# A VectorE exp built from four tensors instead of three, in a kernel that adds attention and a gated MLP

## Chip, cores, metric

One core of a Trainium2 chip. The experiments ran on several chips; each is compared with the kernel before on its own chip, in the same rounds. The metric is the time on the device in microseconds (us), median of several executions. Engines: PE is TensorE (PEld its weight load), DVE is VectorE, ACT is ScalarE, POOL is GpSimd.

## The reference

```python
def _A_ref(x, wqkv, wo):                    # x: 1 x 2048 x 512, 32 heads of 16
    qkv = (x @ wqkv).reshape(B, S, 3, H, Dh).transpose(2, 0, 3, 1, 4)
    scores = einsum("bhqd,bhkd->bhqk", q, k) * (Dh ** -0.5)
    p = softmax(scores)
    return (p @ v).transpose(...).reshape(B, S, D) @ wo
def _B_ref(x, W_gate, W_up, W_down):        # inner width 1792
    return (relu(x @ W_gate) * (x @ W_up)) @ W_down
xn = layernorm(x)
return x + _A_ref(xn, ...) + _B_ref(xn, ...)
```

There are 32 x 2048 x 2048 exps, cut into 2048 tiles of 128 x 512. Nothing else in the program is as large.

## The kernel before

The program describes all its work as operations with durations, priorities and dependencies; a list scheduler in the kernel puts them in one fixed order per engine, and the order is then emitted. A change of a duration, a count or a constant therefore gives a new order of everything.

ACT does the exp of most tiles, in units of alternately three and two tiles, from five PSUM banks that TensorE fills with scores:

```python
SIZES = (3, 2)
...
G.op("PE", 225, sc, mode="row", rows=[t[4] for t in cl], reads=rd, writes=[ts], prio=u - 2000, ...)
...
return e.activation(ring[:, a:a + n, :], ps_sc[:, 3 * k0:3 * k0 + n, :], ACTF.Exp, scale=0.25)
```

98 groups of four tiles go to VectorE, which builds exp from the bits of a bf16 number. Each d1 turns one tile of scores into a bit pattern; d2 to d5 work on the group at once:

```python
# d1, four times: pattern = score * a + b, written as uint16
e.tensor_scalar(dring[:, tr.slot, 0, 512*j:512*j+512].bitcast(U16), ps_b[:, 2, :], 0.25*LOG2E*128.0, ..., op0=ALU.mult, op1=ALU.add)
# d2: mantissa, d3: exponent with a small constant, d4: mantissa squared, d5: pattern times the square
e.tensor_scalar(b(2, U16), b(0, U16), 0x7F, 0x3F80, op0=ALU.bitwise_and, op1=ALU.bitwise_or)
e.tensor_scalar(b(1, U16), b(0, U16), 0xFF80, N_MANT, op0=ALU.bitwise_and, op1=ALU.bitwise_or)
e.tensor_tensor(b(2, FP16), b(2), b(2), ALU.mult)
e.tensor_tensor(b(2), b(0), b(2, FP16), ALU.mult)
```

The weighted sum of the three tensors is never formed. TensorE multiplies each with its own scaled copy of v and adds them in PSUM, so such a group costs it three PV steps (probabilities times v; one step is four column-tiled matmuls), where a group of ACT's costs one. Holes in TensorE's order are filled with dummy matmuls on zeros.

The softmax here doesn't subtract the row's maximum and nothing guards it: scores larger than these inputs give would overflow.

## Time and profile before

| | before |
|---|---|
| time, median | 784.8 us (784.17 to 785.02) |
| profiled span, mean clock | 781.5 us, 0.999 |
| busy PE / DVE / ACT | 757.5 / 734.8 / 762.6 us |

A line of the costliest groups gives source line, engine, operation, out<-in with shapes and count; then busy time and the mean ns of one; then the idle time before them and what ended most of it. The stage lines give, for a stretch in us, each engine's busy time and count, the clock, the DMA share and GB/s. The prediction below shows both.

### The profile page before, as it was taken

The page shows a single profiled execution, that of the slowest core. Times are in us where ns is not written, and L with a number is a line of the kernel's source. Part 1 is how long each engine was busy: PE and PEld are TensorE (multiplying, and loading weights), DVE is VectorE, ACT ScalarE, POOL GpSimd, SP SyncE. Part 2 cuts the span into 40 slices and gives each one's busy share as a digit, 9 for nine tenths or more (in the row PEclk, how much of TensorE's full clock was granted, in tenths as well). Part 3 has the DMA queues.
Part 4 walks back from the last instruction along what each step waited for, and adds up shares of the span by engine and source line. Part 5 has one row for each costly group of instructions (what it writes and reads, how often), then busy time and mean ns, then how long its engine had stood idle before and what let it go on. Part 6 is the DMA issues. An engine that isn't in the chain of part 4 may idle for free.

```text
span 781.5 us, 20994 instructions
## 1 busy us (share of the span) xinstructions
PE 757.5 (97%) x9226; PEld 225.6 (29%) x9226; DVE 734.8 (94%) x1068; ACT 762.6 (98%) x678; POOL 165.5 (21%) x172
## 2 busy tenths in 40 slices
PE   8999999999999999999999999999999999999997
PEld 3322222222222222222222222222222232322232
DVE  8689999999999999999999899999999998999894
ACT  6999999999999999999999999999999999999995
POOL 3111122220222213121222021222021131221200
PEclk9999999999999999999999999999999999999999
DMA  7312121212220132221221113121213113321100
GB/s 215 111 40 71 41 65 41 63 36 66 53 76 23 43 83 56 64 53 47 68 57 56 42 43 84 42 74 38 70 41 83 49 29 96 78 76 43 31 20 28
DMA packets 95755, 46.80 MB, mean 60 GB/s; under 512 B 69936, under 2 KB 91824, under 8 KB 95664
## 3 DMA queue, kind: packets, MB, share of 16 engines
q1 hardware_dynamic: 95664, 45.46, 21.5%
q8 instruction: 72, 1.18, 0.6%
q14 instruction: 19, 0.16, 0.1%
HBM read 36.70 MB, written 8.50 MB: 58 GB/s over the span
## 4 chain that ended last, share of the span: by engine, by line
DVE 52%; PE 35%; ACT 10%; DMA 1%; issue 1%; POOL 0%; DVEq 0%; SPq 0%
DVE dring L1193 17%; PE ps_b L707 13%; ACT ring L1245 10%; PE ps_sc L1177 9%; DVE dring L1209 8%; PE ps_b L1153 8%; DVE dring L1210 8%; DVE dring L1205 4%; DVE dring L1207 4%; DVE up_sb L923 3%; PE ps_b L1177 3%; DVE hT L927 3%; DVE Wv L1089 1%; PE ps_b L1295 1%; DVE stats L616 1%
## 5 line engine op out<-in xcount | busy, mean ns | idle before, releaser
L1245 ACT ACTIVATE ring<-ps_sc 128x1536 bf16<-128x1536 f32 (+1 forms) x663 | 754.4, 1281 | 2.9 <-PE ps_sc L1177 1.4
L1193 DVE TENSOR_SCALAR dring<-ps_b 128x512 uint16<-128x512 f32 x392 | 267.3, 682 | 20.7 <-PE ps_b L1177 20.3
L1177 PE MATMUL ps_sc<-qm,kT 32*128 32x512 bf16 x1656 | 263.8, 384 | 6.0 <-ACT ring L1245 3.5
L1177 PE MATMUL ps_b<-qm,kT 32*128 32x512 bf16 x392 | 150.0, 383 | 5.6 <-DVE dring L1193 3.3
L1153 PE MATMUL ps_b<-ring,v_aug 128*17 128x512 bf16 x1656 | 149.2, 382 | 2.2 <-DVE Wv L1089 1.2
L1107 POOL TENSOR_TENSOR rrec<-rsum,minus 128x16 f32<-128x16 f32 x30 | 100.2, 3341 | 229.1 <-DMA rsum<-Wv 229.1
L1177 PEld LDWEIGHTS ps_sc<-qm,kT 32*128 32x128 bf16 x1656 | 63.5, 91 | 233.3 <-ACT ring L1245 203.9
L1210 DVE TENSOR_TENSOR dring<-dring 128x2048 bf16<-128x2048 bf16 x98 | 118.9, 1213 | 0.1
L1209 DVE TENSOR_TENSOR dring<-dring 128x2048 f16<-128x2048 bf16 x98 | 118.9, 1213 | 0.0
L1117 POOL TENSOR_TENSOR x_sb<-Wv,rb 128x128 bf16<-128x128 f32 x100 | 45.7, 457 | 280.0 <-DVE dring L1207 89.8
L707 PE MATMUL ps_b<-xnT,wus 128*32 128x512 bf16 x896 | 69.1, 384 | 0.8 <-DVE hT L927 0.2
L1205 DVE TENSOR_SCALAR dring<-dring 128x2048 uint16<-128x2048 uint16 x98 | 67.3, 687 | 1.5
L707 PE MATMUL ps_b<-xnT,wgs 128*32 128x512 bf16 x896 | 67.6, 384 | 0.4 <-DVE up_sb L923 0.2
L1207 DVE TENSOR_SCALAR dring<-dring 128x2048 uint16<-128x2048 uint16 x98 | 66.9, 683 | 0.0
L1153 PE MATMUL ps_b<-dring,vd 128*17 128x512 bf16 x784 | 64.9, 381 | 0.0
L707 PE MATMUL ps_b<-Wd,hT 128*32 128x512 bf16 x768 | 58.9, 382 | 0.1
L1153 PEld LDWEIGHTS ps_b<-ring,v_aug 128*17 128x17 bf16 x1656 | 36.9, 89 | 68.2 <-issue 50.1
L1177 PEld LDWEIGHTS ps_b<-qm,kT 32*128 32x128 bf16 x392 | 35.6, 91 | 57.9 <-DVE dring L1193 43.8
L923 DVE COPY up_sb<-ps_b 128x512 f32<-128x512 f32 x56 | 38.1, 680 | 1.8 <-PE ps_b L707 1.8
L1153 PE MATMUL ps_b<-dring,v_aug 128*17 128x512 bf16 x392 | 38.5, 383 | 1.3 <-DVE dring L1207 0.6
L1295 PE MATMUL ps_b<-zeros 128*17 128x512 bf16 x460 | 39.1, 381 | 0.0
L927 DVE SCALAR_TENSOR_TENSOR hT<-ps_b,up_sb 128x512 bf16<-128x512 f32 x48 | 32.7, 680 | 0.0
(106 smaller groups left out, 356.2 us busy)
## 6 DMA issues: line engine op xcount, KB each, us to landing
rb<-rec_scr SPq DMA_DIRECT2D x30, 256.0 KB
wus<-in_B_W_up_dram SPq DMA_DIRECT2D x56, 128.0 KB, 3.5
wgs<-in_B_W_gate_dram SPq DMA_DIRECT2D x56, 128.0 KB, 2.3
qm<-q_scr SPq DMA_DIRECT2D x30, 128.0 KB
o_scr<-x_sb SPq DMA_DIRECT2D x25, 128.0 KB
q_scr<-qT SPq DMA_DIRECT2D x17, 128.0 KB
xr_sb<-in_A_x_dram SPq DMA_DIRECT2D x16, 128.0 KB, 2.8
out_dram<-xn_sb SPq DMA_DIRECT2D x16, 128.0 KB, 1.7
```

What stands on the lines that cost most here:

```text
L707: ins = e.matmul(bank_of(tile, sub)[32 * j:32 * j + 32, :], st[:, 32 * j:32 * j + 32], mv, start=(i == 0), stop=(i == n - 1), tile_positio ...
L923: G.op("DVE", 610, lambda e: e.tensor_copy(up_sb[:, tup.slot, :], bank_of(tu)), reads=[tu], writes=[tup], prio=slots[1] + EV)
L927: G.op("DVE", 610, lambda e: e.scalar_tensor_tensor(out=h_of(th), in0=bank_of(tg), scalar=0.0, in1=up_sb[:, tup.slot, :], op0=ALU.max, op1 ...
L1107: G.op("POOL", 3000, lambda e: e.tensor_tensor(rrec[:, par, :], rsum[:, par, :], minus[:, 0:1].to_broadcast([128, 16]), ALU.pow), reads=[t ...
L1153: ins = e.matmul(ps_b[32 * j:32 * j + VN, 0, :], v, src[j][1](k), start=(first and k == 0), stop=(last and (k == 2 or not on)), tile_posit ...
L1177: return e.matmul(bank, kT[32 * j:32 * j + 32, gg, 128 * kt:128 * kt + 128], qm[32 * j:32 * j + 32, t_q[(c4, gg)].slot, ee, :], start=True ...
L1193: o = G.op("DVE", 610, lambda e, j=j: e.tensor_scalar(dring[:, tr.slot, 0, 512 * j:512 * j + 512].bitcast(U16), ps_b[:, 2, :], 0.25 * LOG2 ...
L1205: G.op("DVE", 600, lambda e: e.tensor_scalar(b(2, U16), b(0, U16), 0x7F, 0x3F80, op0=ALU.bitwise_and, op1=ALU.bitwise_or), reads=[tr], wri ...
L1207: G.op("DVE", 600, lambda e: e.tensor_scalar(b(1, U16), b(0, U16), 0xFF80, N_MANT, op0=ALU.bitwise_and, op1=ALU.bitwise_or), reads=[tr], w ...
L1209: G.op("DVE", 1140, lambda e: e.tensor_tensor(b(2, FP16), b(2), b(2), ALU.mult), reads=[tm], writes=[tm], prio=u - 3, name="d4", lock=True)
L1210: G.op("DVE", 1140, lambda e: e.tensor_tensor(b(2), b(0), b(2, FP16), ALU.mult), reads=[tm, tr], writes=[tm], prio=u - 3, name="d5", lock= ...
L1245: return e.activation(ring[:, a:a + n, :], ps_sc[:, 3 * k0:3 * k0 + n, :], ACTF.Exp, scale=0.25)
```

## The change

The intent: drop the squaring, one of the two dear two-input operations, by using the raw mantissa integer as a factor, and pay for the accuracy with a fourth cheap tensor and a fourth PV step. The freed VectorE time takes six more groups from ACT (98 to 104).

```diff
-NDR = 3
+NDR = 9
-D_GROUPS = 98
-D_SKIP = 12
+D_GROUPS = 104
+D_SKIP = 10
-O_LAST = 58
+O_LAST = 70
-EV = -940.0
-PACE_L = 1.2
+EV = -20.0
+PACE_L = 1.1
...
-    SLIP = 200.0
-    KEEP = 6.0
-    RIDE = 40.0
+    SLIP = 60.0
+    KEEP = 4.0
+    RIDE = 70.0
...
-        dring = sb("dring", [128, NDR, 3, 4 * 512], BF16)
+        dring = sb("dring", [128, NDR, 4 * 512], BF16)
...
-            for k in range(3 if on else 1):
+            ways = len(src[0][0])
+            for k in range(ways):
+                rd = [t_vones, t_v[kt]] + ([t_vd[kt]] if k > 1 else [])
...
-            G.op("DVE", 600, lambda e: e.tensor_scalar(b(2, U16), b(0, U16), 0x7F, 0x3F80, op0=ALU.bitwise_and, op1=ALU.bitwise_or),
-            G.op("DVE", 600, lambda e: e.tensor_scalar(b(1, U16), b(0, U16), 0xFF80, N_MANT, op0=ALU.bitwise_and, op1=ALU.bitwise_or),
-            G.op("DVE", 1140, lambda e: e.tensor_tensor(b(2, FP16), b(2), b(2), ALU.mult), ...
-            G.op("DVE", 1140, lambda e: e.tensor_tensor(b(2), b(0), b(2, FP16), ALU.mult), ...
+            G.op("DVE", 600, lambda e: e.tensor_scalar(b(tm, U16), b(tp, U16), 0xFF80, None, op0=ALU.bitwise_or),
+            G.op("DVE", 600, lambda e: e.tensor_scalar(b(tn, U16), b(tp, U16), 0xFF80, 1, op0=ALU.bitwise_and, op1=ALU.bitwise_or),
+            G.op("DVE", 1140, lambda e: e.tensor_tensor(b(tm), b(tp), b(tm, I16), ALU.mult), ...
+            G.op("DVE", 600, lambda e: e.tensor_scalar(b(ts_, U16), b(tp, U16), float(SHIFT), None, op0=ALU.add),
```

More of the change, by code (lines that the diff above doesn't have):

```diff
@@ L8 @@
 I32 = mybir.dt.int32
+I16 = mybir.dt.int16
 U16 = mybir.dt.uint16
@@ L51 @@
 O_END = 74
-O_LAST = 58
+O_LAST = 70
 O_BEG = 24
-EV = -940.0
-PACE_L = 1.2
+EV = -20.0
+PACE_L = 1.1
 LOG2E = 1.4426950408889634
-W_N = 0.5
-N_MANT = 124
-W_T = 0.1640625
-W_SUM = 2.1484825774371074
-LOG2_SUM = 1.1033182
+SHIFT = 36
+W_T = 1.0 / 256.0
+W_S = 0.0859375
+LOG2_SUM = 0.6922224415
 NUP = 1
@@ L805, in proj_v @@
                 tvd = t_vd[kt] = Tile("vd")
-                for k, w in ((0, W_N), (1, W_T)):
+                for k, w in ((0, W_T), (1, W_S)):
                     G.op("DVE", 230, lambda e, k=k, w=w: e.tensor_scalar(
@@ L1142, in pv_group @@
             first, last = kt == first_kt[key], kt == last_kt[key]
-            rd = [t_vones, t_v[kt]] + ([t_vd[kt]] if on else [])
-            for tr, _ in src:
-                if tr not in rd:
-                    rd.append(tr)
-            for k in range(3 if on else 1):
+            ways = len(src[0][0])
+            for k in range(ways):
+                rd = [t_vones, t_v[kt]] + ([t_vd[kt]] if k > 1 else [])
+                for tr, _ in src:
+                    if tr[k] not in rd:
+                        rd.append(tr[k])
                 def pv(e, k=k):
@@ L1151, in pv @@
                     for j in range(4):
-                        v = v_aug[:, kt, 8 * gg + 2 * j + ee, 0:VN] if k == 0 else vd[:, KD.index(kt), k - 1, 8 * gg + 2 * j + ee, 0:VN]
+                        v = v_aug[:, kt, 8 * gg + 2 * j + ee, 0:VN] if k < 2 else vd[:, KD.index(kt), k - 2, 8 * gg + 2 * j + ee, 0:VN]
                         ins = e.matmul(ps_b[32 * j:32 * j + VN, 0, :], v, src[j][1](k), start=(first and k == 0),
-                                       stop=(last and (k == 2 or not on)), tile_position=(0, 32 * j))
+                                       stop=(last and k == ways - 1), tile_position=(0, 32 * j))
                     return ins
@@ L1161, in pv_group @@
                     o.order.difference_update(mine)
-                    o.order.update(mine if last and k == (2 if on else 0) else mine[:1])
+                    o.order.update(mine if last and k == ways - 1 else mine[:1])
                 if first and k == 0:
                     G.ops[-1].opens = ("pv", [G.ops[-1]])
-                if last and k == (2 if on else 0):
+                if last and k == ways - 1:
                     G.ops[-1].opens = ()
@@ L1182, in dve_exp @@
         def dve_exp(g, u):
-            tr = Tile("dr", P_dr)
+            tp, tm, tn, ts_ = (Tile("dr", P_dr) for _ in range(4))
             t4 = [g + (j,) for j in range(4)]
@@ L1190, in dve_exp @@
                      prio=u + D_WAIT, name="dsc", after=u - 3, order=prev_d)
-                G.ops[-1].acq.append(tr)
+                G.ops[-1].acq.append(tp)
                 mine.append(G.ops[-1])
-                o = G.op("DVE", 610, lambda e, j=j: e.tensor_scalar(dring[:, tr.slot, 0, 512 * j:512 * j + 512].bitcast(U16), ps_b[:, 2, :],
+                o = G.op("DVE", 610, lambda e, j=j: e.tensor_scalar(dring[:, tp.slot, 512 * j:512 * j + 512].bitcast(U16), ps_b[:, 2, :],
                                                                     0.25 * LOG2E * 128.0, 128.0 * (127.0 - LOG2_SUM), op0=ALU.mult, op1=ALU.add),
-                         reads=[ts], writes=[tr], prio=u - 960, name="d1")
@@ L1196, in dve_exp @@
-                for w in tr.w[:-1]:
+                         reads=[ts], writes=[tp], prio=u - 960, name="d1")
+                for w in tp.w[:-1]:
                     o.deps.pop(w, None)
-                if tr in o.acq:
-                    o.acq.remove(tr)
+                if tp in o.acq:
+                    o.acq.remove(tp)
             last_d[:] = mine
-            def b(k, dt=BF16):
-                return dring[:, tr.slot, k, :].bitcast(dt) if dt is not BF16 else dring[:, tr.slot, k, :]
@@ L1204, in dve_exp @@
-            tm, tn = Tile("dm"), Tile("dn")
-            G.op("DVE", 600, lambda e: e.tensor_scalar(b(2, U16), b(0, U16), 0x7F, 0x3F80, op0=ALU.bitwise_and, op1=ALU.bitwise_or),
-                 reads=[tr], writes=[tm], prio=u - 3, name="d2", lock=True)
-            G.op("DVE", 600, lambda e: e.tensor_scalar(b(1, U16), b(0, U16), 0xFF80, N_MANT, op0=ALU.bitwise_and, op1=ALU.bitwise_or),
-                 reads=[tr], writes=[tn], prio=u - 2.5, name="d3", lock=True)
-            G.op("DVE", 1140, lambda e: e.tensor_tensor(b(2, FP16), b(2), b(2), ALU.mult), reads=[tm], writes=[tm], prio=u - 3, name="d4", lock=True)
@@ L1210, in dve_exp, with b @@
-            G.op("DVE", 1140, lambda e: e.tensor_tensor(b(2), b(0), b(2, FP16), ALU.mult), reads=[tm, tr], writes=[tm], prio=u - 3, name="d5", lock=True)
-            tr.w.extend(tn.w + tm.w)
+            def b(t, dt=BF16):
+                return dring[:, t.slot, :].bitcast(dt) if dt is not BF16 else dring[:, t.slot, :]
+            G.op("DVE", 600, lambda e: e.tensor_scalar(b(tm, U16), b(tp, U16), 0xFF80, None, op0=ALU.bitwise_or),
+                 reads=[tp], writes=[tm], prio=u - 3, name="d2", lock=True)
@@ new lines, in dve_exp @@
+            G.op("DVE", 600, lambda e: e.tensor_scalar(b(tn, U16), b(tp, U16), 0xFF80, 1, op0=ALU.bitwise_and, op1=ALU.bitwise_or),
+                 reads=[tp], writes=[tn], prio=u - 2.5, name="d3", lock=True)
+            G.op("DVE", 1140, lambda e: e.tensor_tensor(b(tm), b(tp), b(tm, I16), ALU.mult), reads=[tm, tp], writes=[tm], prio=u - 3, name="d5", lock=True)
+            G.op("DVE", 600, lambda e: e.tensor_scalar(b(ts_, U16), b(tp, U16), float(SHIFT), None, op0=ALU.add),
+                 reads=[tp], writes=[ts_], prio=u - 2.4, name="d4", lock=True)
@@ L1212, in dve_exp @@
             for i in range(4):
-                where[g + (i,)] = (tr, lambda k, i=i: dring[:, tr.slot, k, 512 * i:512 * i + 512])
+                where[g + (i,)] = ((tp, tn, tm, ts_), lambda k, i=i: dring[:, (tp, tn, tm, ts_)[k].slot, 512 * i:512 * i + 512])
         dve_todo = [(max(0.0, at_group[g] - D_LEAD), g) for g in groups if g in on_dve]
@@ L1247, in bass_parallel_sum__mha_block__glu_gated_reglu__prompt_kernel @@
             for i, t in enumerate(cl):
-                where[t] = (tr, lambda k, tr=tr, i=i, f=ring_of: f(tr, i))
+                where[t] = ((tr,), lambda k, tr=tr, i=i, f=ring_of: f(tr, i))
             while pv_next < len(groups) and all(groups[pv_next] + (j,) in where for j in range(4)):
```

## The prediction

> **What bounds the kernel now.** I began with the page's busy shares (part 1), then the groups by form, because three engines stand above 93% and the share alone does not say which one sets the end.
>
> ```profile
> PE 757.5 (97%) x9226; PEld 225.6 (29%) x9226; DVE 734.8 (94%) x1068; ACT 762.6 (98%) x678; POOL 165.5 (21%) x172
> ...
> L1245 ACT ACTIVATE ring<-ps_sc 128x1536 bf16<-128x1536 f32 (+1 forms) x663 | 754.4, 1281 | 2.9 <-PE ps_sc L1177 1.4
> L1193 DVE TENSOR_SCALAR dring<-ps_b 128x512 uint16<-128x512 f32 x392 | 267.3, 682 | 20.7 <-PE ps_b L1177 20.3
> ...
> L1210 DVE TENSOR_TENSOR dring<-dring 128x2048 bf16<-128x2048 bf16 x98 | 118.9, 1213 | 0.1
> L1209 DVE TENSOR_TENSOR dring<-dring 128x2048 f16<-128x2048 bf16 x98 | 118.9, 1213 | 0.0
> ...
> L1205 DVE TENSOR_SCALAR dring<-dring 128x2048 uint16<-128x2048 uint16 x98 | 67.3, 687 | 1.5
> ...
> L1207 DVE TENSOR_SCALAR dring<-dring 128x2048 uint16<-128x2048 uint16 x98 | 66.9, 683 | 0.0
> ```
>
> ScalarE's exp took 754.4 us and sat idle for only 2.9 us before its 663 instructions. Next the busy time by stage, in stretches of 40 us (columns: PE, PEld, DVE, ACT, POOL busy, then clock, DMA share, GB/s):
>
> ```profile
> 200.00:240.00 40.00, 38.76 (x453) 11.11 (x451) 39.60 (x56) 39.98 (x36) 9.12 (x10) 1.00 0.23 61
> ...
> 600.00:640.00 40.00, 39.69 (x513) 12.01 (x513) 37.55 (x54) 39.65 (x36) 6.56 (x9) 1.00 0.16 45
> ```
>
> ACT is full in all of them from 40 us on. The timeline says where its chain begins and ends: the first exp starts at 10.46, and the last group of five starts at 767.03 and takes 5.18.
>
> ```profile
> 10.46 2.51 ACT L1245 ACTIVATE ring<-ps_sc 128x1536 bf16<-128x1536 f32 x2 [0.58 <-PE ps_sc L1177]
> ...
> 767.03 5.18 ACT L1245 ACTIVATE ring<-ps_sc 128x1536 bf16<-128x1536 f32 x5
> ```
>
> So the span is 10.5 us of start, 761.8 us of ACT stream, and 781.5 - 772.2 = 9.3 us of tail (last PV, normalisation, output). In the stream stand 754.4 us of exp and, from the groups by form, 2.3 + 2.0 + 2.0 us of V, K and transpose evictions: 760.7, or all but about 1 us. **ACT sets the end**, and the chain of waits, which gives DVE 52% and PE 35%, must not be read as a ranking: in a program in which all wait for all, it follows whichever came last.
>
> PE is the hidden second bound. A busy PE is not a full one, so I read starts in the timeline instead:
>
> ```profile
> 641.22 0.39 PE L1153 MATMUL ps_b<-ring,v_aug 128*17 128x512 bf16 x4
> ...
> 641.43 0.39 PE L707 MATMUL ps_b<-Wo,x_sb 128*32 128x512 bf16 x4
> ...
> 641.75 0.39 PE L1177 MATMUL ps_sc<-qm,kT 32*128 32x512 bf16 x2
> ...
> 642.07 0.40 PE L707 MATMUL ps_b<-Wo,x_sb 128*32 128x512 bf16 x4
> ```
>
> Four column-tiled matmuls are one step, and steps follow at 0.21 to 0.22 us; a turn to the row-tiled scores costs 0.32, and the turn back 0.32. This repeats with hardly a hole. What PE has spare is shown by its dummy matmuls on zeros (460, so 115 steps), which fill holes:
>
> ```profile
> L1295 PE MATMUL ps_b<-zeros 128*17 128x512 bf16 x460 | 39.1, 381 | 0.0
> ```
>
> At 0.22 us that is 25 us. By stretch (busy time of that line alone) they lie at 4.36 us in 80 to 120 and 4.17 in 320 to 360, but 0.39 in 600 to 640 and none from 640 to 760: the last quarter has no filling left to give.
>
> **What the skill says.** "VectorE: DVE Perf Modes", section "The perf-mode tier table", gives 693 ns for a 2048-element 16-bit tensor_scalar from SBUF and 1224 ns for tensor_tensor; the trace agrees (683 to 687, and 1213). "Vector Engine (DVE) Microarchitecture Reference", section 5.1, makes the two-element mode depend on 2-byte dtypes throughout, not on equal ones. The trace agrees for a mixed pair: bf16 in, fp16 out costs 1213 like all bf16. So I take bf16 times int16 at 1213 and the uint16 add at 685; no row here shows either. "TensorEngine Tiling (Array Packing)", section "Key Properties", says that a change of tiling mode drains the array; the trace has the 0.32 against 0.22. "Perfetto Trace Analysis", under the per-instruction lifecycle, says a matmul's end is estimated; hence starts, not ends, above.
>
> **The change, part by part.**
>
> DVE. A group of 4 score tiles had four evictions, two bit operations and two products. In the timeline the starts are closer than the durations: 0.60 us after a tensor_scalar, 1.13 to 1.14 after a product. That is 6 x 0.60 + 2 x 1.135 = 5.87 us. The change replaces the squaring by one more tensor_scalar: 7 x 0.60 + 1.135 = 5.34 us. In all 98 x 5.87 = 575 against 104 x 5.34 = 555 us: DVE gets about 20 us lighter (734.8 to some 715) though it does six groups more. DVE was not the bound, so this buys nothing by itself; it allows the six groups.
>
> ACT. Six groups leave it: 24 of 1656 tiles, so 1632 in 653 units. A pair of units (five tiles) costs 754.4 / 331.2 = 2.278 us, a tile 0.4556; 24 x 0.4556 = 10.9 us. This is the only gain on the path. Nothing in the diff touches the start or the tail.
>
> PE. Each DVE group now needs four PV steps instead of three: 104 x 4 - 98 x 3 = 416 - 294 = +122, less six groups of one step on the ACT side: +116 steps x 0.22 = +25.5 us. Ten units fewer save ten visits to row mode, each 0.32 + 0.32 - 0.22 = 0.42: -4 us; 24 more score tiles for DVE, of which about half ride with another row visit, cost +3 us. Net about +25 us, which is the whole of the dummies, in a stream 11 us shorter. Counting starts over the trace, I find some 38 us in which steps come later than 0.22 or 0.32 apart. So PE had 25 + 38 = 63 us of slack in the 762 us stream, and will have 63 - 25 - 11 = 27 us in 751. In 640 to 760, where there are no dummies, the late steps were about 1.1 us in each 40, 3%; 3% of 751 is 20 us. So PE can just serve ACT on average, with little to spare, and less than that in the last quarter: it gains 26 x 4 - 24.5 x 3 - 1.5 = 29 steps, 6.4 us, and has 2.7 us less time, against some 7 us of slack in 580 to 760. I expect ACT to be kept waiting there, and to lose 1 to 3 us. The wider riding of score tiles (40 to 70) and the longer spread of the output projection (58 to 70) push the other way; they are timings of the scheduler, and I can't count them without building.
>
> Buffers. Nine single planes replace three triples, the same memory. A group now holds four planes, each freed after its own PV step. In-flight groups fall from 3 to 9 / 4 = 2.25, but PV may start on the bit pattern at once rather than after the last product, and the first two tensors need no scaled v.
>
> Sum: 784.8 - 10.9 = 773.9 us if ACT stays full; plus about 2 us of waits for PE: **776.0 us**.
>
> **Rivals.** (1) ACT stays full and the whole 10.9 us comes home: 774. For it: ACT 39.65 to 39.97 even in the stretches where PE had no dummies. Against: those stretches now get more PV. (2) PE becomes the bound: if late steps stay at 38 us rather than shrink, 25 + 38 - 11 - 25 leaves PE 11 us short, and the time comes back to 784 or 785; a poor order of PE's queue (six other scheduling constants change at once) might even cost more. For it: the 97%, and the last quarter; against: 38 us contains holes that arose just because PE had nothing to do. (3) The planes become the wait: the first score of a group can't be taken until a plane is free, DVE starts late, PV of DVE groups comes late and holds the PV accumulator. The rows speak little for it: DVE's wait for those scores is 20.3 us in all, and DVE gains about 10 us of slack. It would give 778 to 790. (4) The product with int16 runs at one element a cycle: by the skill's 2293 ns for that mode, 104 x about 1.07 us = 111 us more on DVE, 826 us of DVE work and a time above 830. The mixed-dtype row speaks against it; I give it 2%.
>
> **Range and chances.** Below, the ACT floor of 774 holds unless the exp itself were faster; nothing suggests it, so the low end is 773. Above, a partial PE bound, 8 us over my centre: 783. Faster by over 2% would need under 769.1, which is 5 us below the floor: 3%. Slower by over 2% is above 800.5, only by rival 4 or a bad order: 4%. Within 2%: 93%.
>
> **What will show it.** ACT exp at 743 to 744 us in 653 instructions; the squaring row gone, three tensor_scalar rows near 685 and one product near 1213 in 104 each; DVE busy near 715; 1632 matmuls of ring tiles and 1664 of DVE tiles in PV; dummies down from 460 to under 150, those left outside the last quarter. ACT's idle before exp should rise from 2.9 to some 3 to 6 us, released by PE scores, mostly after 580 us. If idle is below 2 us, rival 1 holds; above 8, rival 2. If DVE idles before L1193's successor for much over 20 us and the planes' readers release it, rival 3. A start later than 10.5 or a tail other than 9.3 us would be a thing I have not foreseen.

## The result, and the profile after

The changed kernel took 777.61 us (777.28 to 777.84, 4 runs) where the kernel before took 784.91 in the same rounds. A ratio here is the mean time of one kernel's fast runs over that of the other's fast runs of the same rounds, so not quite the ratio of the medians: 0.9908, 95% interval 0.9891 to 0.9925: a gain clear of noise, and inside the 2% band to which the prediction gave 93%. The profiled span went from 781.5 to 775.5 us.

From the page of the changed kernel (busy shares, then groups):

```profile
PE 759.1 (98%) x9330; PEld 228.2 (29%) x9330; DVE 720.8 (93%) x1116; ACT 755.3 (97%) x668; POOL 161.2 (21%) x172
...
L1246 ACT ACTIVATE ring<-ps_sc 128x1536 bf16<-128x1536 f32 (+1 forms) x653 | 747.2, 1258 | 4.2 <-PE ps_sc L1179 1.2
L1195 DVE TENSOR_SCALAR dring<-ps_b 128x512 uint16<-128x512 f32 x416 | 284.1, 683 | 30.2 <-PE ps_b L1179 27.2
...
L1210 DVE TENSOR_TENSOR dring<-dring 128x2048 bf16<-128x2048 bf16 x104 | 126.2, 1213 | 0.0
...
L1211 DVE TENSOR_SCALAR dring<-dring 128x2048 uint16<-128x2048 uint16 x104 | 71.1, 684 | 0.0
```

The squaring is gone, the product with the integer costs the same 1213 ns and the new add 684. The idle time before the exps rose by only 1.3 us. Yet their busy time fell by 7.2 us, not by the 10.9 that 24 tiles are worth. Dummies (groups by form of the changed kernel) fell from 460 matmuls to 100, that is from 115 steps to 25, all of them before 580 us:

```profile
L1296 PE MATMUL ps_b<-zeros 128*17 128x512 bf16 x100 | 8.4, 382 | 0.0
```

Where are the missing 3 to 4 us, when ACT is busy all the time? **In starts that busy time does not show.** The starts in the trace say that an exp follows a two-tile exp at best 904 ns after its start, and a three-tile one at 1331 to 1348 ns; but their records last about 1020 to 1100 and 1450 to 1530 ns. So consecutive records overlap by some 0.1 us, and an exp can start that much late while the sum of busy time shows no gap. I call lateness the distance of two starts beyond 904 or 1348 ns, summed over the kernel; it is a count from the starts in the trace. Before it was 19.1 us, in the changed kernel 23.2. (Some 6.0 us of each, the same in every run, are no late exps: ScalarE's own evictions stand between exps in the first 35 us.) The stream, from the first exp's start to the last one's end, went from 761.8 to 755.7 us: the exps account for -10.9, lateness for +4.1, and 0.8 remain as the error of the sum. Start and tail are as they were (10.46 us and 9.3 us).

Apart from those evictions, the lateness lies almost wholly before three-tile exps (17.3 us of it), whose scores must be made in the 0.9 us of a two-tile exp. The trace shows what came in between. From the 31st exp on, 16.6 us of lateness stand before three-tile exps of the changed kernel; for 13.7 of them one step of four matmuls, and for 2.5 two steps, started between the bank's coming free (the end of the exp two before) and its first score. The last step in front was a PV step of a VectorE group for only 3.5 us; for 5.4 it was a PV step of ScalarE's own groups, for 6.7 a step of the MLP or of the attention's projections. That fits added steps which delay by filling the queue, and seldom by standing in front themselves. The view of waits shows how often TensorE stood ready. Before (engine, output and line, what it waited for, total us, times, longest):

```profile
PEld ps_sc L1177 <- ACT ring L1245: 203.9, 510, 0.9
...
PEld ps_sc L1177 <- issue: 26.1, 92, 0.4
```

And the changed kernel:

```profile
PEld ps_sc L1179 <- ACT ring L1246: 186.3, 470, 0.7
...
PEld ps_sc L1179 <- issue: 35.8, 129, 0.4
```

A wait of TensorE for ACT is good here: the score was at the head of the queue when its bank came free. That fell from 510 of 663 turns (a turn is the scores of one exp) to 470 of 653. "issue" is a turn in which nothing had to be waited for, because ACT had freed the bank earlier and TensorE was still in other work: 92 to 129. From the median three-tile exp's record end to its bank's next score it is 258 ns before and about 300 after.

### The profile page after: what moved, and what is told of

Same layout as the page of the kernel before. It is cut to its first block, busy times and chain, and to the rows that moved or that the text cites. A ratio compares the mean times of both kernels' runs of the same rounds, so it can differ in the third digit from the quotient of the medians.

```text
span 775.5 us, 21246 instructions
## 1 busy us (share of the span) xinstructions
PE 759.1 (98%) x9330; PEld 228.2 (29%) x9330; DVE 720.8 (93%) x1116; ACT 755.3 (97%) x668; POOL 161.2 (21%) x172
## 4 chain that ended last, share of the span: by engine, by line
PE 69%; DVE 27%; ACT 2%; issue 0%; DMA 0%; POOL 0%; DVEq 0%
PE ps_b L707 24%; PE ps_b L1155 20%; PE ps_sc L1179 19%; DVE dring L1195 9%; PE ps_b L1179 6%; DVE dring L1210 4%; DVE dring L1206 3%; ACT ring L1246 2%; DVE dring L1208 2%; DVE dring L1211 2%; DVE up_sb L923 1%; DVE Wv L1089 1%; DVE hT L927 1%; DVE stats L616 1%; DVE v_aug L801 1%; DVE kT L790 1%
## 5 line engine op out<-in xcount | busy, mean ns | idle before, releaser
L1246 ACT ACTIVATE ring<-ps_sc 128x1536 bf16<-128x1536 f32 (+1 forms) x653 | 747.2, 1258 | 4.2 <-PE ps_sc L1179 1.2
L1195 DVE TENSOR_SCALAR dring<-ps_b 128x512 uint16<-128x512 f32 x416 | 284.1, 683 | 30.2 <-PE ps_b L1179 27.2
L1179 PE MATMUL ps_sc<-qm,kT 32*128 32x512 bf16 x1632 | 259.2, 384 | 2.6 <-ACT ring L1246 1.3
L1179 PE MATMUL ps_b<-qm,kT 32*128 32x512 bf16 x416 | 159.3, 383 | 1.3 <-DVE dring L1195 0.9
L1107 POOL TENSOR_TENSOR rrec<-rsum,minus 128x16 f32<-128x16 f32 x30 | 95.1, 3171 | 230.4 <-DMA rsum<-Wv 230.4
L1210 DVE TENSOR_TENSOR dring<-dring 128x2048 bf16<-128x2048 bf16 x104 | 126.2, 1213 | 0.0
L1155 PE MATMUL ps_b<-dring,vd 128*17 128x512 bf16 x832 | 74.2, 381 | 0.8 <-DVE dring L1211 0.4
L1155 PE MATMUL ps_b<-dring,v_aug 128*17 128x512 bf16 x832 | 74.8, 382 | 0.0
L1206 DVE TENSOR_SCALAR dring<-dring 128x2048 uint16<-128x2048 uint16 x104 | 72.0, 692 | 2.3
L1211 DVE TENSOR_SCALAR dring<-dring 128x2048 uint16<-128x2048 uint16 x104 | 71.1, 684 | 0.0
L1208 DVE TENSOR_SCALAR dring<-dring 128x2048 uint16<-128x2048 uint16 x104 | 71.0, 683 | 0.0
L1155 PEld LDWEIGHTS ps_b<-ring,v_aug 128*17 128x17 bf16 x1632 | 36.8, 89 | 68.6 <-issue 48.0
L1155 PEld LDWEIGHTS ps_b<-dring,vd 128*17 128x17 bf16 x832 | 18.7, 88 | 33.7 <-issue 12.0
```

The source lines that it names most:

```text
L1107: G.op("POOL", 3000, lambda e: e.tensor_tensor(rrec[:, par, :], rsum[:, par, :], minus[:, 0:1].to_broadcast([128, 16]), ALU.pow), reads=[t ...
L1155: ins = e.matmul(ps_b[32 * j:32 * j + VN, 0, :], v, src[j][1](k), start=(first and k == 0), stop=(last and k == ways - 1), tile_position=( ...
L1179: return e.matmul(bank, kT[32 * j:32 * j + 32, gg, 128 * kt:128 * kt + 128], qm[32 * j:32 * j + 32, t_q[(c4, gg)].slot, ee, :], start=True ...
L1195: o = G.op("DVE", 610, lambda e, j=j: e.tensor_scalar(dring[:, tp.slot, 512 * j:512 * j + 512].bitcast(U16), ps_b[:, 2, :], 0.25 * LOG2E * ...
L1206: G.op("DVE", 600, lambda e: e.tensor_scalar(b(tm, U16), b(tp, U16), 0xFF80, None, op0=ALU.bitwise_or), reads=[tp], writes=[tm], prio=u - ...
L1208: G.op("DVE", 600, lambda e: e.tensor_scalar(b(tn, U16), b(tp, U16), 0xFF80, 1, op0=ALU.bitwise_and, op1=ALU.bitwise_or), reads=[tp], writ ...
```

## The experiments

Theory A: the added PV steps stand in TensorE's queue in front of scores and make exps late. Rivals: B, the six other constants cost it; C, the planes (nine single buffers in place of three triples) are a new wait; D, the order of the queues sets it and TensorE's load as such doesn't. "Late" is split below at 500 ns: small ones, as a column step of 0.22 us in front would give, and holes. Of the evictions' 6.0 us, 4.5 stand among the holes and 1.4 among the small ones of every run: the kernel before has no other hole. The last three columns are of the profiled execution, which was the slowest of its four in the runs with three PV steps, with the new constants on the kernel before, and without dummies. The levels of lateness in the expectations differ from the table's (20 us for the changed kernel, here 23.2); what can be compared is the changes.

| run | ratio to before | late, up to 500 ns | holes over 500 ns | clock |
|---|---|---|---|---|
| before | 1 | 14.5 | 4.5 | 0.999 |
| changed | 0.9908 | 18.1 | 5.1 | 0.999 |
| changed, three PV steps, re-ordered | 0.9937 | 18.0 | 10.0 | 0.995 |
| before, fourth PV step, re-ordered | 1.0153 | 16.6 | 14.2 | 1.000 |
| four tensors, 98 groups, re-ordered | 1.0096 | 18.4 | 8.6 | 0.992 |
| changed with old constants, re-ordered | 0.9984 | 17.3 | 11.8 | 0.999 |
| changed, short fourth step, same order | 0.9869 | 14.8 | 5.1 | 1.000 |
| before, extra fourth step, same order | 1.0142 | 25.5 | 4.5 | 1.000 |
| before with 104 groups, re-ordered | 1.0308 | 11.9 | 41.4 | 0.999 |
| before with new constants, re-ordered | 1.0033 | 16.5 | 6.8 | 0.997 |
| before, no dummies, same order | 1.0211 | 16.8 | 20.2 | 0.961 |
| changed, no dummies, same order | 0.9965 | 18.9 | 10.1 | 0.988 |
| before, light squaring, same order | 0.9952 | 11.2 | 5.6 | 1.000 |
| retimed | 0.9890 | 10.0 | 7.1 | 0.999 |

### First four: each in a new order

```diff
-            ways = len(src[0][0])
+            ways = min(3, len(src[0][0]))
```

> The changed kernel (104 groups, all four VectorE tensors computed) without the fourth PV step; the result is wrong on purpose. 104 steps of 0.22 us = 23 us of TensorE work less than the changed kernel. Theory A (the lost 5 us of the 10.9 us are exps that start late because TensorE's queue has more PV steps in it): the stream of exps comes back to about its floor, 773.5 to 775.5 us, late exps back under 14 us by start-to-start. Theory B (the other constants of the scheduler cost it): stays near 777.6. Theory C (planes): about 776 to 777.6, since only the fourth plane is freed sooner.

Measured: 779.13 us, ratio 0.9937 (0.9921 to 0.9954; the changed kernel's interval ends at 0.9925): most likely slower than the changed kernel, though TensorE had 23 us less to do. (The comparison with the reference still passed; its tolerance does not notice the fourth tensor.) All three theories missed. By stage, in the stretch at 360 to 440 us:

```profile
360.00:400.00 40.00, 38.64 (x432) 10.54 (x424) 37.61 (x56) 39.11 (x35) 9.04 (x10) 0.96 0.21 55
400.00:440.00 40.00, 39.23 (x471) 10.86 (x471) 36.97 (x55) 38.26 (x34) 7.62 (x8) 0.96 0.20 53
```

The clock was halved there for 6.8 us and ACT ran out of work, 39.11 and 38.26 of 40. That is not the whole of it: this was the slowest execution (781.46 us), the other three kept a clock of 0.998 to 0.999 and took 778.64 to 779.40, and in this one ACT had only 38.18 of 40 us at full clock from 720 to 760. The order had changed with the step, and the constants had been tuned to another; which of these did it is not shown.

```diff
-            for k in range(3 if on else 1):
+            for k in range(4 if on else 1):
...
+                        v = ... zeros[:, 0:VN] if k == 3 else ...
```

> The kernel before with a fourth PV step per VectorE group, on zero weights, so the result is unchanged: 98 steps of 0.22 us = 22 us more for TensorE, nothing for ScalarE or VectorE. Theory A: 2.5 to 5 us slower than before, 787 to 790 us, ScalarE's exp count and floor unchanged, late exps up by the same. Theory B or C: 784.5 to 785.5, the step only takes the place of a dummy.

Measured: 795.84 us, ratio 1.0153, much slower than A expected, mostly in holes (4.5 to 14.2 us). I took this at first for the new order's doing.

```diff
-D_GROUPS = 104
-D_SKIP = 10
+D_GROUPS = 98
+D_SKIP = 12
```

> The new four-tensor form with the old number of groups (98, skip 12). ScalarE has the same 1656 tiles as before, VectorE is about 52 us lighter, TensorE has 98 more PV steps. Theory A: no gain from the lighter VectorE, a loss of 1 to 4 us from the PV steps: 785 to 789 us. If a lighter VectorE itself were worth something (my prediction said nothing), it would be under 784.

Measured: 791.56 us, ratio 1.0096; above A's range, clock 0.992. The four-tensor form without the six groups is a loss. But order, clock and load are mixed here.

```diff
-O_LAST = 70
-EV = -20.0
-PACE_L = 1.1
+O_LAST = 58
+EV = -940.0
+PACE_L = 1.2
-    SLIP = 60.0
-    KEEP = 4.0
-    RIDE = 70.0
+    SLIP = 200.0
+    KEEP = 6.0
+    RIDE = 40.0
```

> The changed kernel (104 groups, four tensors) with the six scheduling constants of before (slip 200, keep 6, ride 40, eviction -940, spread 58, pace 1.2). Theory A with the constants a small help: 777.5 to 781 us. Theory B (the constants are what cost the 5 us): 774 to 776.

Measured: 782.69 us, ratio 0.9984, slower even than A expected. With the old constants the change is worth next to nothing; so **B as stated falls**: the constants did not cost the missing us, they keep holes out (11.8 us of them without, 5.1 with). These four taught that a re-ordered kernel doesn't measure one cost. The next ones hold every queue's order, checked instruction by instruction.

### The same order, less or more work for TensorE

```diff
-ins = e.matmul(ps_b[32*j:32*j+VN, 0, :], v, src[j][1](k), ...
+ins = e.matmul(ps_b[32*j:32*j+VN, 0, 0:32 if k == 3 and not last else 512], v, src[j][1](k)[:, 0:32 if k == 3 and not last else 512], ...
```

> The changed kernel, every queue in exactly its order and with all its waits, but the fourth PV step of a VectorE group moves 32 columns instead of 512 (wrong on purpose): 20 us of TensorE work taken away and nothing else. The first four runs were each put in a new order by the program's scheduler, which brought long holes of their own; this one holds the order. Theory A (more PV steps on TensorE make the exps of three tiles start late): late exps fall from 20 us towards 16 us by start-to-start, ratio to before 0.985 to 0.989 (773 to 776 us). Theory D (the order of the queues sets it, TensorE's load as such doesn't): ratio 0.990 to 0.992, as the changed kernel.

Measured: 773.74 us, ratio 0.9869 (0.9847 to 0.989), within A's range. Lateness fell from 23.2 to 20.0 us, all of it in the small ones, and the stream to 751.8 us. The page:

```profile
PE 749.5 (97%) x9330; PEld 228.2 (30%) x9330; DVE 719.7 (93%) x1116; ACT 752.2 (97%) x668; POOL 163.0 (21%) x172
...
L1246 ACT ACTIVATE ring<-ps_sc 128x1536 bf16<-128x1536 f32 (+1 forms) x653 | 744.0, 1281 | 3.4 <-PE ps_sc L1179 1.6
```

ACT's exps now take 744.0 us, the floor that the prediction worked out. The mean record is back at 1281 ns: its records are longer when the input already waits, so **a falling mean with a full engine is a sign of lateness** (1281 before, 1258 changed, 1281 here). With all planes, constants and waits in place, 20 us of PV work cost this kernel about 0.4%, 3 us (the two intervals just miss each other). C has little left to explain.

```diff
-                                       stop=(last and (k == 2 or not on)), ...)
+                                       stop=(last and not on), ...)
+                    for j in range(4 if k == 2 else 0): ins = e.matmul(ps_b[32*j:32*j+VN, 0, :], zeros[:, 0:VN], src[j][1](k), start=False, stop=last, ...)
```

> The kernel before in exactly its order, with four zero-weight matmuls added behind each VectorE group's third PV step, result unchanged: 98 x 0.22 = 22 us more TensorE work at unchanged order, where the earlier run with a fourth PV step was re-ordered and came out 11.8 us slower. Theory A: 4 to 8 us slower than before (ratio 1.005 to 1.010), in late exps of 100 to 300 ns. Theory D: under 2 us slower (below 1.0025), so that nearly all of the 11.8 us were the new order.

Measured: 795.22 us, ratio 1.0142: beyond A's range on the slow side, and D is out. Lateness rose by 11 us, wholly in the small ones (14.5 to 25.5), so half of the added 22 us of PE work came through to the time. The waits show the same:

```profile
PEld ps_sc L1178 <- ACT ring L1246: 171.0, 429, 0.9
...
PEld ps_sc L1178 <- issue: 58.5, 171, 0.4
```

It corrects my reading of the second run: at the old order a fourth step costs as much as at a new one, in small latenesses instead of holes. Here the bill was the load, and the order decided in which coin it was paid; the first run shows that an order can also cost by itself. It also shows that the dummies do not step aside: they stood in the order and stayed.

### Was six more groups possible without the new form?

```diff
-D_GROUPS = 98
-D_SKIP = 12
+D_GROUPS = 104
+D_SKIP = 10
```

> The kernel before (three tensors, four post operations with the squaring) with 104 groups on VectorE and skip 10. VectorE then has about 35 us more work, 770 of some 774 us. My account: VectorE becomes the bound, and the six groups bring nothing: 790 to 812 us, with VectorE over 97% busy and ScalarE idle for 15 us or more. If instead VectorE has room, 775 to 780.

Measured: 808.61 us, ratio 1.0308. As expected in time, with ACT idle before its exps for 36.8 us; but VectorE was 95% busy, not over 97%. The waits of ACT in this run:

```profile
ACT ring L1245 <- PE ps_b L1153: 28.2, 17, 4.5
ACT ring L1245 <- PE ps_sc L1177: 7.6, 6, 3.9
```

Seventeen holes of up to 4.5 us behind PV steps. That VectorE's late tensors held those PV steps is my reading of them and not shown. VectorE was full (39.97 of 40 us) in three stretches where ACT lost much, 160 to 200, 320 to 360 and 720 to 760, but at 35.5 to 38.0 in three others; that the order was not tuned for it may count too.

```diff
-O_LAST = 58
-EV = -940.0
...
+O_LAST = 70
+EV = -20.0
...
```

> The kernel before with the six scheduling constants of the changed one, 98 groups. If the constants are an improvement by themselves: under 783. If they fit only the changed kernel (what I expect, since the old ones cost the changed kernel 5 us in the run with the old constants): 785 to 790.

Measured: 787.09 us, ratio 1.0033, as expected. Each set of constants fits its own kernel.

### Are the dummies in the way?

```diff
-        G.fill = {"pv": blank_pv, ...}
+        fill_ = {"pv": blank_pv, ...}
```

> The kernel before without its dummy matmuls in the stream, every other instruction of every queue in the same order: 115 steps, 25 us of TensorE work away. Theory A (any step in front of a score delays an exp, dummy or not; 22 us added cost 10.4 us): 2 to 5 us faster than before, ratio 0.993 to 0.997, late exps from 19 to 14 to 17 us, unless TensorE's clock drops in the holes, when it would be slower and the granted clock below 0.99. Theory A' (dummies lie only where nothing waits): within 0.2% of before.

Measured: 801.98 us, ratio 1.0211 (1.017 to 1.0253). Two stretches of it, and beneath them the same of before:

```profile
160.00:200.00 40.00, 38.33 (x448) 10.98 (x448) 39.17 (x57) 39.90 (x36) 8.85 (x10) 1.00 0.18 47
...
520.00:560.00 40.00, 38.05 (x390) 10.09 (x390) 37.49 (x53) 37.53 (x33) 10.51 (x9) 0.90 0.22 55
```

```profile
160.00:200.00 40.00, 39.17 (x464) 11.15 (x468) 39.17 (x56) 39.90 (x36) 9.17 (x10) 1.00 0.17 46
...
520.00:560.00 40.00, 38.48 (x442) 10.82 (x442) 39.65 (x56) 40.00 (x36) 10.55 (x10) 1.00 0.18 47
```

At full clock, up to 200 us, ACT has the same 39.90 with and without dummies, and the 161st exp starts at 199.2 us with them and at 199.4 without: the 22 steps up to there lie where nothing waits, so A' is right as to that. Later the clock halves for stretches of 3.4 to 13.7 us and ACT starves. The skill's "TensorE: Matmul & The Clock Gate", section "What's actually happening", says that throttled is the default state and that activity releases it; this run agrees (mean clock 0.961). So the dummies cost nothing that shows up to there, and over the whole kernel they save 17 us.

> The changed kernel without its 25 dummy steps, order otherwise the same: 5.5 us of TensorE work away. Theory A: up to 1 us faster than the changed kernel, ratio to before 0.989 to 0.991. Theory A': unchanged, 0.9908. A drop of the clock: slower.

The edit is the same, on the changed kernel. Measured: 781.86 us, ratio 0.9965 (0.9935 to 0.9995), clock 0.988: slower, by the clock. The four executions took 783.16, 782.97, 780.76 and 778.19 us at clocks of 0.988, 0.988, 0.992 and 0.998. Its 25 dummy steps, 5.5 us, hold 4 us.

### Does a lighter VectorE bring something by itself?

```diff
-e.tensor_tensor(b(2, FP16), b(2), b(2), ALU.mult)
+e.tensor_scalar(b(2, FP16), b(2), 1.0, None, op0=ALU.mult)
```

> The kernel before in exactly its order, with the squaring replaced by a product with 1.0 of the one-input kind (wrong on purpose): VectorE is 98 x 0.53 = 52 us lighter, TensorE and ScalarE have the same work, and nothing else moves. My prediction said that a lighter VectorE buys nothing by itself: 783 to 785 us, ratio 0.998 to 1.0. If VectorE's tensors hold TensorE's queue, and so the exps, it should be 3 us faster or more (ratio below 0.996) with late exps well under 19 us.

Measured: 780.29 us, ratio 0.9952 (0.9935 to 0.9968), result wrong (relative error 0.022). Late small ones fell from 14.5 to 11.2 us, and TensorE stood ready for ACT at 575 turns instead of 510:

```profile
PEld ps_sc L1177 <- ACT ring L1245: 236.0, 575, 0.9
...
PEld ps_b L1177 <- DVE dring L1193: 22.9, 69, 0.7
```

The same wait for VectorE in the kernel before:

```profile
PEld ps_b L1177 <- DVE dring L1193: 43.8, 120, 0.8
```

So 52 us off VectorE are worth 3 to 4 us although VectorE doesn't bound the kernel: TensorE, in a fixed order, waits less for VectorE to empty its score bank (22.9 us instead of 43.8), and comes to its scores in time. "Nothing" was wrong.

### A version with durations from the trace

```diff
-D_GROUPS = 104
-D_LEAD = 9.0
-EV = -20.0
-PACE_L = 1.1
-    RIDE = 70.0
-    LAT = {"PE": 150.0, "ACT": 220.0, ...}
-G.op("ACT", 75 + 427 * n, ex, ...)
+D_GROUPS = 101
+D_LEAD = 10.0
+EV = -40.0
+PACE_L = 1.0
+    RIDE = 100.0
+    LAT = {"PE": 190.0, "ACT": 168.0, ...}
+G.op("ACT", 31 + 436 * n, ex, ...)
```

> A version that may beat both: the new tensors with 101 groups instead of 104 (12 PV steps less, 3 x 4 tiles more for ScalarE, 5.4 us of exps), and the scheduler given durations as the traces show them (exps 1339 and 903 ns start to start instead of 1356 and 929, shorter release, longer way from score to exp), with lead 10, ride 100, eviction -40, pace 1.0. Theory A: late exps fall by more than the 5.4 us of exps cost; 771 to 777 us. If durations in the scheduler don't matter: 778 to 784.

Measured: 775.26 us (775.22 to 775.66), result correct, ratio 0.9890 (0.9875 to 0.9904), within A's range. Its page:

```profile
L1246 ACT ACTIVATE ring<-ps_sc 128x1536 bf16<-128x1536 f32 (+1 forms) x658 | 746.0, 1361 | 3.4 <-PE ps_b L1155 2.2
```

Five more exps than the changed kernel and still less busy time; the mean of 1361 ns says that most inputs waited for ACT. Lateness is 17.1 us against 23.2. Its median is the best of all versions that compute the whole exp. The two ratios' intervals overlap, so its lead over the changed kernel is likely and not shown. Which of its edits brings it was not taken apart.

## Why the prediction was right or wrong

The time (776.0 said, 777.6 measured) and the range held. By its steps:

- **ACT sets the end, and 24 tiles are the gain.** Right. With the fourth steps short, the exps took 744.0 us, the floor worked out beforehand, and the ratio was 0.9869 where the floor of 773.9 over 784.8 says 0.986. But that floor is no floor: 0.4556 us a tile is the mean of the kernel before, lateness included. The retimed version's 1644 tiles took 746.0 us where this rate gives 749.0.
- **Durations of the new operations.** Right: 692, 683 and 684 for the one-input ones, 1213 for bf16 times int16. Rival 4 is out. VectorE's busy time came to 720.8, not 715.
- **TensorE can just serve ACT, and loses 1 to 3 us.** Right in mechanism, somewhat small in size. Lateness rose by 4.1 us; the short fourth step removes 3.2 of them. The step that sized it assumed slack to be used up before anything is lost. The same-order runs speak against that: by the prediction's own count 22 us more would have left the kernel before 63 - 22 = 41 us of slack, and they cost 11; 20 us removed from the changed kernel gave 3. That so little was lost in the changed kernel also owes to what the prediction said it couldn't count: with the old constants the same change took 782.69 us. So the closeness of the 776.0 is partly luck.
- **Mostly after 580 us.** Wrong: 1.7 of the 4.1 us of lateness came there, from counting starts, which is more than the quarter's share, but most is spread over the kernel. It is not a quarter running full but a step of 0.22 us standing in front of a score, anywhere.
- **ACT's idle would tell (3 to 6 us).** It read 4.2, inside the band, but it was the wrong witness. It rose by 1.3 us while lateness rose by 4.1, since overlapping records hide a start that is up to 0.1 us late. For that reason the expected exp busy of 743 to 744 read 747.2.
- **A lighter VectorE buys nothing by itself.** Wrong: 52 us of it bought 3 to 4 us in the kernel before at unchanged order. How much of the change's own 14 us came through this way no run separates.
- **Dummies make room.** Right in count (460 to 100), and none after 580 us; but what they do is hold the clock, which the prediction passed over.
- **Rival 2's sum.** 25 + 38 - 11 - 25 is 27, not 11 short; 11 short comes out only if the 38 us can't be used at all and are left out. (A small slip besides: 1.1 us in each 40 is 2.75%, and that makes the 20 us.)
- **Planes (rival 3).** Not tried alone. DVE's wait for scores rose from 20.3 to 27.2 us, TensorE's scores ending it; with the planes unchanged the short fourth step came down to 20.0 us of lateness, 0.9 above before, which leaves little for it as a wait. Whether fewer groups in flight shaped the order itself, no run tests.

## What to carry to other kernels

In this kernel with three nearly full engines, work added to the second bound cost a part of itself at once (11 of 22 us, 3 of 20); count it, even where average slack seems to cover it. When a program orders its queues by a scheduler, test a cost at unchanged order (shorten or lengthen an instruction in place), because a re-ordered kernel measures its tuning as well. Read how full the bounding engine is from start to start, and from how often its feeder had to wait for it, rather than from busy time.

## What the Trainium skill lacked or had wrong

- "Perfetto Trace Analysis", per-instruction lifecycle: it says what a record of ScalarE spans, but no page says that a late start hides where consecutive records overlap, so that busy time doesn't show it. Here exps of two tiles start 904 ns apart at best and last 1017 ns or more, and the mean record of the exps moved between 1255 and 1361 ns with how long inputs had waited.
- "TensorEngine Tiling (Array Packing)", "Key Properties": the drain on a change of tiling mode has no figure. Between the row and column forms here a turn costs 0.32 us start to start against 0.22 within a form.
- "VectorE: DVE Perf Modes", "The perf-mode tier table": the table has no row for mixed 2-byte types; the rule that the prediction drew on covers them, and it held. bf16 times int16 into bf16 took 1213 ns, an add on uint16 684 ns, as the like-typed ones.
- "TensorE: Matmul & The Clock Gate": no page gives a figure for how many short holes, none of them long, bring the clock down. Taking away 115 dummy steps, 25 us spread over a kernel whose TensorE stayed 94% busy by its records, brought the mean clock to 0.961 and the time up by 2.1%. The clock was halved nine times between 210 and 607 us, where no two matmul starts were over 1.30 us apart.
